# Early gate logits for the sixth batch, and separate pools for the value buffers and the raw second weights

## The chip, the cores and the metric

The kernel runs on one core of one Trainium2 chip. A core has a matrix engine (TensorE, PE in the rows; its weight loads are PEld), a vector engine (VectorE, DVE), a scalar engine (ScalarE, ACT), a general engine (GpSimd, POOL) and a queue engine (SyncE, SP) that issues transfers; GpSimd issues transfers too, the indexed ones. Each engine executes its own instructions in order, and waits on semaphores for the others. The metric is the device time of one execution in microseconds, the median of the runs shown.

## What is computed

An attention by landmarks (eight batches, eight heads, 576 positions, 64 channels; 32 landmarks, a pseudo-inverse by six iterations) makes 4608 rows of 512 numbers; a mixture of eight experts takes each row to the one expert with the largest gate logit.

```
attn = (sm(q, k_lm) @ Z @ sm(q_lm, k) @ v)        # Z: six steps of 2Z - Z Bm Z
x = attn.transpose(0, 2, 1, 3).reshape(B * S, H * D)
logits = x @ w_gate
expert_idx = argmax(logits, axis=1); gate_w = softmax(logits)[expert_idx]
for e in range(E):
    mask = expert_idx == e
    h = maximum(x[mask] @ w1[e], 0); out[mask] = gate_w[mask] * (h @ w2[e])
```

## The kernel before

The work has two halves. The attention runs in 18 periods (`period(i)`); a unit is half a batch (four heads). Unit i is loaded and transposed in period i (`front`), multiplied with the landmarks in i + 1 (`middle`), with the values in i + 2 (`values`); the batch's inverse is iterated in periods 2b + 3 and 2b + 4 (`back`: `chain`, its squarings on L321, then `apply`, which makes the tile w on L364), and its rows come out in 2b + 5 and 2b + 6 (`final`). Inside a period the streams are merged, and a scheduler orders the instructions of each engine at build time, so that any change of the text can move others.

`final` (L374 to L400) goes through the six row blocks j of a batch. For each it makes two products of 96 rows by 264 columns (L388): 256 columns of the row and 8 of the gate logits, two banks of PSUM. ACT copies each to `xrow` (L389), DVE copies and adds the logits (L392, L393), SP stores the row block to `xs`. Only after the last block does `tokens` run: it takes the largest logit, counts the tokens of each expert with seven small products (L569 to L572), and makes the places `l_at` (L583) at which six indexed transfers of GpSimd (`scatter`, L594), 96 tokens each, write the token numbers to the table `order`. `scatter` is a list of work that the next period executes.

The last two batches, 6 and 7 (the seventh and eighth), go another way. `logits` (L402) makes the gate logits alone, six products of 192 columns (L411), transposes them on DVE (L415) and runs `tokens` at once, so that the places are known before the rows; `ended` then makes the rows (L432). Behind the periods stands a hand-written part: the fetch of the second weights of the first expert (L783, `raw1`, four transfers of 512 KB), `scattered` for batch 5, then logits, rows and scatters of batch 6, then of batch 7, with the splits of `raw1` (`whi` on ACT L797, `wlo` on DVE L798) and the first slot's expert product (L853) between them. When all scatters have landed, GpSimd gathers the table (L643), PE turns it (L657), and from it the addresses of all later rows come (L821). From there a loop over slots of 128 rows does up product, ReLU, down product.

The tile pools matter in one way. A pool opened where closed pools lay waits for the tiles of all pools that it overlaps. Here `raw1`, `whi1` and `wlo1` are one pool of 48 KB per partition, opened over the load buffers (`a_ld`: `ld_k`, `ld_q`, `ld_v`) and the transposed ones (`T_k`, `T_q`); another, `e_work` (`buf`, `xt`, `xg`, `h`, `ht`), lies over `T_q` and the work tiles of `middle` and `values`. The first write into such a pool therefore waits for the last product of `values` of the last unit (L263).

In what follows a name with a number in brackets is a batch, as w(6), and the squarings of a batch are counted from 0.

Of the kernel before, what the change touches and what calls it, by code (L numbers as in the profile page):

```python
# [12 lines left out]
F32 = mybir.dt.float32  # L13
# [8 lines left out]
B, H, S, D = 8, 8, 576, 64  # L22
M = 32
P96, J = 96, 6
NT = B * S
DM, NE, DF = 512, 8, 1024
# [34 lines left out]
class Attention:  # L61


    def __init__(self, tc, ctx, front, psum, q, k, v, wg):
        self.tc, self.nc = tc, tc.nc
        nc = self.nc
        self.q, self.k, self.v = q, k, v
        pool = lambda n, b, c=ctx: c.enter_context(tc.tile_pool(name=n, bufs=b))
# [5 lines left out]
        self.row = pool("a_row", 3)  # L74
        self.lg = pool("a_lg", 2)
        self.ld = pool("a_ld", 2, front)
        self.tr = pool("a_tr", 2, front)
        self.wk = pool("a_wk", 2, front)
        self.p_tp, self.p_sc, self.p_fr, self.p_ch, self.p_fi = psum
        self.rows, self.loads, self.banks = [], {}, []  # L80
        c = self.const
# [26 lines left out]
    def load(self, i, names):  # L108
        b, g = divmod(i, 2)
        for n in names:  # L110
            t = self.src[i, n] = self.ld.tile([P96, 4, J * D], F32, name=f"ld_{n}")
            m = 2 if i < 2 else 4
            for h in range(0, 4, m):
                self.loads[n] = self.nc.sync.dma_start(out=t[:, h:h + m], in_=getattr(self, n)[b, 4 * g + h:4 * g + h + m].rearrange("h (p j) d -> p h (j d)", j=J))
# [260 lines left out]
    def final(self, b):  # L375
# [24 lines left out]
                yield  # L400
        yield from sort

    def logits(self, b, room):

        nc = self.nc
        ats, w = self.fin[b]
        pl = self.p_fi.tile([128, 512], F32, name="ps_fi")
        for g in range(2):
            at = ats[g].rearrange("p (a b t c) -> p t b a c", a=2, b=J // 2, t=3)
            for t in range(3):  # L410
                nc.tensor.matmul(pl[32 * t:32 * t + 32, :32 * J].rearrange("p (b a c) -> p b a c", a=2, b=J // 2),  # L411
                                 lhsT=w[:, g, QUAD - 32:], rhs=at[:, t], start=g == 0, stop=g == 1, tile_position=(0, 32 * t))
        yield
        lt = room[:P96, :32 * J]
        nc.vector.transpose(out=lt, in_=pl[:P96, :32 * J])  # L415
        yield from self.tokens(b, range(J), lt.rearrange("p (j e) -> p j e", j=J)[:, :, 32 - NE:])
# [22 lines left out]
    def period(self, i, nb, extra=()):  # L439

        n = 2 * nb
# [14 lines left out]
        for lag, stage, units in ((3, self.back, 26), (5, self.final, 20)):  # L456
            b, h = divmod(i - lag, 2)
            if 0 <= b < nb and (lag, b) not in ((3, nb - 1), (5, nb - 2)):
                if h == 0:
                    self.two[lag, b] = stage(b)  # L460
                half = units // 2 + 1
                streams.append((self.part(self.two[lag, b], 99 if h else half), half, BOOST[lag]))
        if i == n:
# [282 lines left out]
class Experts:  # L746
# [11 lines left out]
        self.hi, self.lo = [None, None], [None, None]  # L758

    def weights(self, ctx, i):  # L760
        p = ctx.enter_context(self.tc.tile_pool(name=f"e_w{i}", bufs=1))
        self.raw[i] = p.tile([128, self.chunks[i], self.width[i]], F32, name=f"raw{i}")
        self.hi[i] = p.tile([128, self.chunks[i], self.width[i]], F32R, name=f"whi{i}")
        self.lo[i] = p.tile([128, self.chunks[i], self.width[i]], F32R, name=f"wlo{i}")

# [186 lines left out]
def moe(tc, q, k, v, wg, w1, w2, out):  # L952
    nc = tc.nc
    with ExitStack() as ctx, ExitStack() as late:
# [9 lines left out]
        with ExitStack() as front:  # L964
            attention = Attention(tc, ctx, front, psum, q, k, v, wg)
            attention.tokens, attention.groups = routing.tokens, routing.groups
            attention.xs = [xs[S * b:S * b + S].rearrange("(p j) c -> p j c", j=J) for b in range(B)]
            routing.ident = attention.ident
            routing.room = {EARLY: front.enter_context(tc.tile_pool(name="r_ids", bufs=1)).tile([16, REC * 128], F32, name="ids_early")}
            for i in range(2 * B + 2):  # L970
                extra = []
# [18 lines left out]
        b = B - 1  # L990
# [88 lines left out]
```

## Time and profile before

| | before |
|---|---|
| median of three runs | 688.84 us (688.47 to 696.65) |
| the profiled execution | 688.39 us, of which the span is 686.6 us |
| PE busy | 647.9 us (94%) |
| DVE, ACT, POOL busy | 520.8, 398.9, 343.9 us (76%, 58%, 50%) |
| mean granted TensorE clock | 0.966 |
| chain that ended last | PE 46% of the span (all of it the expert products), DMA 4%, issue 3%, DVE 1%, POOL 1% |

The page's share of busy time averages over two unlike halves: the attention with many short instructions on all engines up to about 250 us, and the expert loop behind it. Times below are microseconds from the start of the span. In a timeline row, the number in square brackets is the engine's idle time ahead of the row and what ended it. Each matrix product of float32 shows as two rows.

### The profile page before, as it was taken

The numbers are of one execution on the slowest core, as the hardware profiler recorded it, in microseconds if no ns is written. First come the engines' busy times: TensorE is split into PE (matmuls) and PEld (weight loads), VectorE is DVE, ScalarE is ACT, GpSimd is POOL, SyncE is SP. The second block draws the span as 40 slices with busy tenths as digits, with TensorE's granted clock in tenths as the row PEclk, the third lists the DMA queues.
The fourth block names the chain that finished last, engine by engine and source line by source line (L and its number), as shares of the span: only waits on it lengthen the run. The fifth ranks groups of instructions, "written<-read, shape, count | busy, mean of one in ns | idle before, by whom it ended". The sixth has DMA issues, their size and how long they took to land.

```text
span 686.6 us, 13812 instructions
## 1 busy us (share of the span) xinstructions
PE 647.9 (94%) x4511; PEld 509.9 (74%) x4511; DVE 520.8 (76%) x1359; ACT 398.9 (58%) x983; POOL 343.9 (50%) x372
## 2 busy tenths in 40 slices
PE   7899989998898996989999999999999999999996
PEld 4666767666576774768888888888888888888884
DVE  4887967989778677668689699866789699766753
ACT  5776667575645373345567567554567567444542
POOL 4554556575364273777545546344444536441231
PEclk9998999998879897999999999999999999999999
DMA  9996877776442441273145143211144143310110
GB/s 228 294 279 160 207 187 171 178 197 200 111 120 65 137 132 43 73 258 112 62 163 176 56 158 117 107 52 49 45 169 157 59 158 107 118 48 32 32 51 30
DMA packets 46362, 87.50 MB, mean 127 GB/s; under 512 B 7983, under 2 KB 26415, under 8 KB 46192
## 3 DMA queue, kind: packets, MB, share of 16 engines
q1 hardware_dynamic: 36336, 65.30, 33.1%
q0 software_dynamic: 9920, 21.02, 9.7%
q8 instruction: 38, 0.62, 0.4%
q14 instruction: 68, 0.56, 0.3%
HBM read 64.77 MB, written 22.05 MB: 126 GB/s over the span
## 4 chain that ended last, share of the span: by engine, by line
PE 46%; DMA 4%; issue 3%; DVE 1%; POOL 1%; ACT 0%; POOLq 0%; DVEq 0%
PE ps_fi L853 12%; PE ps_ch L853 12%; PE ps_tp L853 11%; PE ps_fr L853 11%; DMA xg<-xs,read 4%; DVE h L873 0%; POOL out_dram L884 0%; POOL xg L821 0%; DVE buf L834 0%; DVE ht L839 0%; ACT ht L836 0%; POOLq L919 0%; POOLq L884 0%; DVEq L834 0%; DVEq L810 0%
## 5 line engine op out<-in xcount | busy, mean ns | idle before, releaser
L884 POOL DMA_INDIRECT out_dram<-buf,write x38 | 38.8, 1020 | 166.4 <-ACTq L810 140.7
L821 POOL DMA_INDIRECT xe<-xs,read x84 | 87.5, 1042 | 25.7 <-issue 24.1
L821 POOL DMA_INDIRECT xg<-xs,read x80 | 83.7, 1046 | 31.3 <-issue 21.8
L853 PE MATMUL ps_fr<-whi,ht 128*128 128x512 f32 x304 | 96.4, 398 | 0.0
L853 PE MATMUL ps_ch<-whi,ht 128*128 128x512 f32 x304 | 94.3, 391 | 2.2 <-ACTq L810 2.2
L836 ACT CAST ht<-buf 128x512 fp32r<-128x512 f32 x76 | 47.1, 621 | 74.9 <-DVE buf L834 73.9
L873 DVE TENSOR_SCALAR h<-ps_tp 32x256 f32<-32x256 f32 x152 | 64.1, 422 | 27.5 <-PE ps_tp L853 25.0
L853 PE MATMUL ps_tp<-whi,xt 128*128 128x512 f32 x304 | 83.2, 395 | 1.5 <-ACTq L810 1.5
L873 DVE TENSOR_SCALAR h<-ps_fi 32x256 f32<-32x256 f32 x144 | 60.7, 422 | 28.9 <-PE ps_fi L853 26.5
L871 ACT ACTIVATE h<-ps_tp 32x256 f32<-32x256 f32 x152 | 57.3, 377 | 36.6 <-PE ps_tp L853 32.9
L853 PE MATMUL ps_fi<-whi,xt 128*128 128x512 f32 x288 | 78.1, 393 | 0.0
L871 ACT ACTIVATE h<-ps_fi 32x256 f32<-32x256 f32 x144 | 54.3, 377 | 34.8 <-PE ps_fi L853 31.1
L853 PEld LDWEIGHTS ps_ch<-whi,ht 128*128 128x128 f32 x304 | 56.9, 188 | 15.2 <-ACTq L810 3.1
L853 PEld LDWEIGHTS ps_fr<-whi,ht 128*128 128x128 f32 x304 | 58.0, 191 | 13.1 <-DVE ht L839 0.5
L853 PEld LDWEIGHTS ps_tp<-whi,xt 128*128 128x128 f32 x304 | 56.9, 188 | 14.3 <-ACTq L810 1.9
L853 PEld LDWEIGHTS ps_fi<-whi,xt 128*128 128x128 f32 x288 | 54.1, 188 | 11.8
L853 PE MATMUL ps_fr<-wlo,ht 128*128 128x512 f32 x152 | 60.4, 397 | 0.0
L594 POOL DMA_INDIRECT order<-i_tok,l_at x48 | 45.7, 952 | 27.7 <-issue 11.5
L853 PE MATMUL ps_ch<-wlo,ht 128*128 128x512 f32 x152 | 59.4, 391 | 0.0
L839 DVE TENSOR_TENSOR ht<-buf,ht 128x512 fp32r<-128x512 f32 x76 | 51.0, 691 | 3.8 <-ACT ht L836 0.2
L798 DVE TENSOR_TENSOR wlo<-raw,whi 128x512 fp32r<-128x512 f32 (+1 forms) x64 | 49.8, 833 | 4.8 <-ACT whi L797 2.4
L834 DVE STREAM_TRANSPOSE buf<-h 128x512 f32<-128x512 f32 x76 | 49.7, 692 | 4.9 <-DMA out_dram<-buf,write 1.0
(274 smaller groups left out, 1325.2 us busy)
## 6 DMA issues: line engine op xcount, KB each, us to landing
raw<-in_moe_w_dram SPq DMA_DIRECT2D x48, 512.0 KB, 5.3
ld_k<-in_k_dram SPq DMA_DIRECT2D x14, 576.0 KB, 5.9
ld_q<-in_q_dram SPq DMA_DIRECT2D x14, 576.0 KB, 7.4
ld_v<-in_v_dram SPq DMA_DIRECT2D x14, 576.0 KB, 4.9
xs<-xrow SPq DMA_DIRECT2D x40, 192.0 KB, 3.3
order<-zero SPq DMA_DIRECT2D x8, 288.0 KB, 9.5
xe<-xs,read POOLq DMA_INDIRECT x84, 2.8
xg<-xs,read POOLq DMA_INDIRECT x80, 2.6
```

The costliest lines, as they stand in the source:

```text
L594: self.nc.gpsimd.indirect_dma_start(out=self.places[n + j], out_offset=bass.IndirectOffsetOnAxis(ap=at[:, j:j + 1], axis=0), in_=self.tok[ ...
L798: (engine or nc.vector).tensor_tensor(out=l, in0=x, in1=h.bitcast(F32), op=ALU.subtract)
L821: self.nc.gpsimd.indirect_dma_start(out=x[:, t, :], out_offset=None, in_=src.rearrange("n (q c) -> (n q) c", q=4), in_offset=bass.Indirect ...
L834: nc.vector.transpose(out=x.rearrange("p c (t j) -> p t c j", t=4), in_=src[:, :, 32 * c:32 * c + 128].rearrange("p t (c i) -> p t c i", c=4))
L836: nc.scalar.copy(out=hi[:, c:c + 4, :], in_=x)
L839: nc.vector.tensor_tensor(out=lo[:, c:c + 4, :], in0=x, in1=hi[:, c:c + 4, :].bitcast(F32), op=ALU.subtract)
L853: nc.tensor.matmul(ps[c // 512] if type(ps) is list else ps[:, c // 512], lhsT=x0[:, a, :], rhs=w[:, a, c:c + 512], start=a == 0 and j == ...
L871: nc.scalar.activation(out=dst, in_=src, func=AF.Relu)
L873: nc.vector.tensor_scalar(out=dst, in0=src, scalar1=0.0, scalar2=None, op0=ALU.max)
L884: nc.gpsimd.indirect_dma_start(out=self.outs[s], out_offset=bass.IndirectOffsetOnAxis(ap=at, axis=0), in_=y, in_offset=None, bounds_check= ...
```

## The change

Batch 5's rows come from a new function, `sorted`, in place of `final`: first the logits alone (`logits`, six products of 192 columns into one bank), then the six row blocks, each with two products of 256 columns into one bank, one copy by ACT of 512 columns instead of two of 256, and one step of `tokens` behind each block. The 12 small copies and adds of DVE are gone; one transpose by DVE into a small tile (`a_room`) stands for them. `tokens` of batch 5 now ends during period 15, so its scatters fall to period 16 instead of the hand-written part. The value buffers get a pool of their own (`a_lv`), and `raw1` one apart from `whi1` and `wlo1`. No tile but `ids_early` changes its address (by 768 bytes); `raw1` lies over `ld_k` and `ld_q` as before, but now waits only for the pool of these two.

```
         self.ld = pool("a_ld", 2, front)
+        self.lv = pool("a_lv", 2, front)
...
-            t = self.src[i, n] = self.ld.tile([P96, 4, J * D], F32, name=f"ld_{n}")
+            t = self.src[i, n] = (self.lv if n == "v" else self.ld).tile([P96, 4, J * D], F32, name=f"ld_{n}")
...
+    def sorted(self, b, room):
+
+        nc = self.nc
+        sort = self.logits(b, room)
+        next(sort)
+        yield
+        ats, w = self.fin.pop(b)
+        for j in range(J):
+            x = self.row.tile([P96, DM], F32, name="xrow")
+            n = self.at_col(j)
+            po = self.p_fi.tile([128, 512], F32, name="ps_fi")
+            for g in range(2):
+                nc.tensor.matmul(po[:P96, 4 * D * g:4 * D * g + 4 * D], lhsT=ats[g][:, n:n + 96], rhs=w[:, g, :4 * D], start=True, stop=True)
+                if g == 0:
+                    yield
+            nc.scalar.copy(out=x.rearrange("p (q c i) -> p c q i", q=4, c=4), in_=po[:P96].rearrange("p (c q i) -> p c q i", c=4, q=4))
+            nc.sync.dma_start(out=self.xs[b][:, j, :], in_=x)
+            next(sort, None)
+            yield
...
-                    self.two[lag, b] = stage(b)
+                    self.two[lag, b] = stage(b) if (lag, b) != (5, nb - 3) else self.sorted(b, self.room)
...
+        p = ctx.enter_context(self.tc.tile_pool(name=f"e_raw{i}", bufs=1))
+        self.raw[i] = p.tile([128, self.chunks[i], self.width[i]], F32, name=f"raw{i}")
         p = ctx.enter_context(self.tc.tile_pool(name=f"e_w{i}", bufs=1))
-        self.raw[i] = p.tile([128, self.chunks[i], self.width[i]], F32, name=f"raw{i}")
...
+            attention.room = front.enter_context(tc.tile_pool(name="a_room", bufs=1)).tile([P96, 32 * J], F32, name="room")
```

Lines of the changed kernel stand 1 to 23 higher: its L432 (logits), L453 (rows of batches 6 and 7), L590 to L593 (counts), L264 (values), L322 (squarings), L856 (turn) are L411, L432, L569 to L572, L263, L321, L834 of before.

PE, from the first product of batch 5's rows in period 15, before:

```order
L388 MATMUL ps_fi<-w,at 96x264
L321 MATMUL ps_ch<-bt 128x160 x2
L388 MATMUL ps_fi<-w,at 96x264
L173 MATMUL ps_sc<-T_q,lm_k 32x288 x8
L125 MATMUL ps_tp<-ident,ld_q 128x96 x3
L271 MATMUL ps_fr<-ident,st 64x128
L125 MATMUL ps_tp<-ident,ld_q 128x96 x3
L388 MATMUL ps_fi<-w,at 96x264
L321 MATMUL ps_ch<-rp 128x128 x2
L125 MATMUL ps_tp<-ident,ld_q 128x96 x3
L277 MATMUL ps_fr<-wg,yt 32x8 x4
L388 MATMUL ps_fi<-w,at 96x264
```

and of the changed kernel:

```order
L432 MATMUL ps_fi<-at,w 32x192 x6
L322 MATMUL ps_ch<-bt 128x160 x2
L416 MATMUL ps_fi<-w,at 96x256 x2
L174 MATMUL ps_sc<-T_q,lm_k 32x288 x6
L126 MATMUL ps_tp<-ident,ld_q 128x96 x3
L174 MATMUL ps_sc<-T_q,lm_k 32x288 x2
L272 MATMUL ps_fr<-ident,st 64x128
L126 MATMUL ps_tp<-ident,ld_q 128x96 x3
L416 MATMUL ps_fi<-w,at 96x256 x2
L322 MATMUL ps_ch<-rp 128x128 x2
L126 MATMUL ps_tp<-ident,ld_q 128x96 x3
L278 MATMUL ps_fr<-wg,yt 32x8 x4
```

The logits stand ahead of everything; further on, up to the products of landmarks of the last unit (L178, L179 of the changed kernel), PE has the seven counts and ten row products instead of six row products ahead of it.

DVE, from the first instruction that writes into `e_work` (`buf` 4091 to 4093 of before), before:

```order
L834 STREAM_TRANSPOSE buf_4091<-xe_144 128x4x4x32
L581 TENSOR_TENSOR l_t<-l_t,l_oh 96x48
L834 STREAM_TRANSPOSE buf_4092<-xe_145 128x4x4x32
L339 TENSOR_TENSOR rp<-rp,ps_tp 128x2x32
L582 TENSOR_REDUCE l_mx<-l_t 96x6
L415 STREAM_TRANSPOSE buf_4093<-ps_fi 96x192
L839 TENSOR_TENSOR xt_4094<-buf_4091,xt_4094 128x512
L583 CAST l_at<-l_mx 96x6
L554 TENSOR_REDUCE l_mx<-buf_4093 96x6
L839 TENSOR_TENSOR xt_4095<-buf_4092,xt_4095 128x512
L555 TENSOR_TENSOR buf_4093<-buf_4093,l_mx 96x6x8
L339 TENSOR_TENSOR rp<-rp,ps_tp 128x2x32
```

and of the changed kernel (L436 is the transpose of logits, here of batch 6; L820 is `wlo`; L340 is L339 of before):

```order
L436 STREAM_TRANSPOSE buf_4091<-ps_fi 96x192
L856 STREAM_TRANSPOSE buf_4089<-xe_144 128x4x4x32
L856 STREAM_TRANSPOSE buf_4090<-xe_145 128x4x4x32
L340 TENSOR_TENSOR rp<-rp,ps_tp 128x2x32
L575 TENSOR_REDUCE l_mx<-buf_4091 96x6
L820 TENSOR_TENSOR wlo_4082<-raw_4077,whi_4081 128x512
L576 TENSOR_TENSOR buf_4091<-buf_4091,l_mx 96x6x8
L820 TENSOR_TENSOR wlo_4082<-raw_4077,whi_4081 128x512
L340 TENSOR_TENSOR rp<-rp,ps_tp 128x2x32
L820 TENSOR_TENSOR wlo_4082<-raw_4077,whi_4081 128x512
```

The transpose of batch 6's logits has moved ahead of the two turns of the first slots, the steps of `tokens` of batch 5 are gone from here, and three subtractions `wlo` have come in ahead of the rest of `tokens` of batch 6; the row that makes its `l_oh` (L564 of before, L585 now) follows after two `xt` subtractions and the two masks L342.

On SP the four transfers of `raw1` stand after the second of the six stores of batch 5 instead of after the sixth, and wait for the last transpose of `ld_q` instead of the last product with `ld_v`. On GpSimd the six scatters of batch 5 stand one `a` product (L236) earlier.

## Rows read from the trace of the kernel before

**Rows 1.** Busy time of each engine by stretches of 50 us: PE, PEld, DVE, ACT, POOL, then granted clock, share of DMA engines, GB/s. One stretch across the join of attention and experts, one of the expert loop.

```profile
250.00:300.00 50.00, 42.80 (x176) 33.37 (x175) 33.67 (x91) 20.20 (x45) 31.45 (x34) 0.90 0.26 74
350.00:400.00 50.00, 50.00 (x220) 40.96 (x219) 42.04 (x79) 31.50 (x68) 23.33 (x22) 1.00 0.39 129
```

**Rows 2.** The chain that ended last, in order of time: first and last of its 58 PE pieces (start, length, what).

```profile
305.42 5.75 PE ps_ch L853 x24
...
619.17 5.53 PE ps_fi L853 x24
```

**Rows 3.** Timeline of PE where the table's transposes stand (start, length, operation).

```profile
264.76 1.07 PE L657 MATMUL ps_fi<-ident,r 43*128 43x43 f32 x4 [5.67 <-DVE r L653]
...
268.48 1.05 PE L853 MATMUL ps_fr<-whi,ht 128*128 128x512 f32 x2
...
269.76 1.05 PE L853 MATMUL ps_fr<-whi,ht 128*128 128x512 f32 x2
...
273.01 0.61 PE L853 MATMUL ps_fr<-whi,ht 128*128 128x512 f32 x2
...
273.69 0.61 PE L853 MATMUL ps_fr<-whi,ht 128*128 128x512 f32 x2
```

**Rows 4.** Stretches around that wait, columns as in rows 1.

```profile
259.00:266.00 7.00, 1.33 (x6) 0.96 (x5) 3.07 (x8) 4.22 (x10) 0.80 (x1) 0.66 0.28 57
266.00:271.00 5.00, 5.00 (x12) 3.60 (x12) 4.63 (x12) 0.00 (x0) 2.91 (x4) 0.50 0.10 30
```

**Rows 5.** Timeline of GpSimd: the first scatter of batch 5, the first and the last of batch 6, the first of batch 7, the gather of the table.

```profile
233.93 1.25 POOL L594 DMA_INDIRECT order<-i_tok,l_at  x1 [10.88 <-DVE l_mx L554]
...
241.60 0.92 POOL L594 DMA_INDIRECT order<-i_tok,l_at  x1 [0.30 <-DVE l_at L583]
...
247.96 1.05 POOL L594 DMA_INDIRECT order<-i_tok,l_at  x1 [0.30 <-issue]
249.32 0.92 POOL L594 DMA_INDIRECT order<-i_tok,l_at  x1 [0.31 <-issue]
...
258.90 0.90 POOL L643 DMA_INDIRECT ht<-order,s_at  x1 [2.17 <-issue]
```

**Rows 6.** Timeline of DVE: the masks of batch 7 and the third squaring's sum of batch 6 behind them, w(6), the first turn, l_oh(6), the first `wlo`, w(7), l_at(7).

```profile
212.15 2.91 DVE L297 TENSOR_TENSOR bt<-bt,m 128x128 f32<-128x128 f32 x2
...
215.93 0.20 DVE L339 TENSOR_TENSOR rp<-rp,ps_ch 128x64 f32<-128x64 f32 x1
...
228.01 0.42 DVE L364 TENSOR_TENSOR w<-ps_ch,m 128x256 f32<-128x256 f32 x1
...
231.07 0.71 DVE L834 STREAM_TRANSPOSE buf<-xe 128x512 f32<-128x512 f32 x1 [2.11 <-PE ps_fr L263]
...
236.35 0.20 DVE L564 TENSOR_TENSOR l_oh<-i_rev,l_m 96x48 bf16<-96x48 f32 x1
...
240.42 0.69 DVE L798 TENSOR_TENSOR wlo<-raw,whi 128x512 fp32r<-128x512 f32 x1 [2.26 <-DMA xs<-xg]
241.03 0.24 DVE L583 CAST l_at<-l_mx 96x6 int32<-96x6 f32 x1
241.10 0.74 DVE L364 TENSOR_TENSOR w<-ps_ch,m 128x256 f32<-128x256 f32 x2
...
248.13 0.16 DVE L583 CAST l_at<-l_mx 96x6 int32<-96x6 f32 x1
```

**Rows 7.** Timeline of PE: landmarks of the last unit, the first three of the twelve rows of logits(6), the last product with the values, rows of batch 6, counts of batch 6, first product behind them, logits(7).

```profile
209.48 0.23 PE L178 MATMUL ps_tp<-lm_k,lm_q 64*32 64x32 f32 x4
...
230.56 0.54 PE L411 MATMUL ps_fi<-at,w 128*32 128x192 f32 x3
230.66 0.31 PE L263 MATMUL ps_fr<-ld_v,ct 96*32 96x64 f32 x1
...
231.99 2.02 PE L432 MATMUL ps_fi<-w,at 128*96 128x256 f32 x4
...
236.69 0.20 PE L569 MATMUL ps_fi<-l_oh,tri 96*96 96x48 bf16 x1
...
243.56 0.85 PE L411 MATMUL ps_fi<-at,w 128*32 128x192 f32 x12
244.34 1.10 PE L432 MATMUL ps_fi<-w,at 128*96 128x256 f32 x4
245.28 1.03 PE L432 MATMUL ps_sc<-w,at 128*96 128x256 f32 x4
```

**Rows 8.** Stretches of the end of the attention, columns as in rows 1.

```profile
227.05:230.45 3.40, 3.40 (x37) 2.98 (x37) 1.86 (x7) 0.17 (x1) 0.00 (x0) 0.50 0.00 0
230.45:233.90 3.45, 3.45 (x20) 1.91 (x20) 2.83 (x10) 1.85 (x4) 0.00 (x0) 0.50 0.44 116
```

**Rows 9.** Groups of instructions on DVE from 229 to 246 us (busy us, mean ns of one, idle ahead).

```profile
L798 DVE TENSOR_TENSOR wlo<-raw,whi 128x512 fp32r<-128x512 f32 x3 | 2.0, 689 | 2.3 <-DMA xs<-xg 2.3
L834 DVE STREAM_TRANSPOSE buf<-xe 128x512 f32<-128x512 f32 x2 | 1.4, 704 | 2.1 <-PE ps_fr L263 2.1
L839 DVE TENSOR_TENSOR xt<-buf,xt 128x512 fp32r<-128x512 f32 x2 | 1.3, 660 | 0.0
```

**Rows 10.** Transfers of the raw second weights: the time from issue to landing, from the view of that tile (225 to 262 us).

```profile
DMA to landing us min/median/max: 3.9/5.4/7.0
```

**Rows 11.** The same for the transfers on the tensor `xs`, 200 to 262 us.

```profile
DMA to landing us min/median/max: 2.1/2.3/3.2
```

## The prediction

> **What bounds the kernel now.** I read the busy time by stretches first. In the expert loop PE is busy all of a stretch at full clock; across the join it misses 7.2 us of 50 [rows 1]. The chain of waits says the same: 58 pieces of expert products follow one another without a gap from 305.42 us to 619.17 + 5.53 = 624.70 [rows 2]. Nothing of the change touches that loop, so its length stays, and the question is only when it begins.
>
> Its beginning hangs on the token table. PE stands still for 5.67 us ahead of the transposes of the table (L657) and resumes at 264.76 [rows 3]. The reader should go back from there on GpSimd: the gather of the table is issued at 258.90, behind the last of six scatters of batch 7, which begin at 249.32 [rows 5]. What the first of these waited for is seen in two rows: l_at(7) is done at 248.13 + 0.16 = 248.29 [rows 6], and GpSimd's last scatter of batch 6 ends at 247.96 + 1.05 = 249.01 [rows 5]. So GpSimd's own queue held it, by 0.7 us only; right behind stands l_at(7). And l_at(7) hangs on PE: from the counts of batch 6 (L569, 236.69) to logits(7) (243.56) PE goes without a gap through rows of batch 6 and first-slot products [rows 7].
>
> The order behind the scatters is the same in both kernels, so the whole execution moves by what the first scatter of batch 7 moves, plus what the clock does on the way. The profiled execution took 688.39 us, 0.45 below the median of 688.84; sums are made against 688.4.
>
> **The change, part by part.**
>
> *Batch 5's scatters leave the tail.* GpSimd is free for 10.88 us ahead of them [rows 5], so they hide in that idle time. This gives the 0.7 us above and no more, because behind it l_at(7) decides.
>
> *The early fetch of raw1.* DVE waits 2.26 us for the landed weights, and w(7) starts only at 241.10 [rows 6]. But w(7) is done at 241.84, and PE reaches logits(7), which reads it, at 243.56 [rows 6, 7]: 1.7 us later, with PE busy in between. I cost this part at nothing; its cover is that slack.
>
> *The smaller work.* The row products shrink from 264 to 256 columns and the small DVE steps go; none of that is on the path alone. Added on PE are the six products for logits(5): 0.85 us at full clock, as logits(7) shows, 1.43 at half, as logits(6) shows (230.56 to 231.99) [rows 7].
>
> *The new order in period 15.* Up to the landmarks of the last unit (L178, 209.48 before) PE now has the logits (1.4), two more pairs of row products (two times 0.94, from the start of one pair at 244.34 to the next at 245.28 [rows 7]) and the counts (0.3 to 0.6) ahead of it: 3.6 to 3.9 us. Batch 7's chain starts that much later, but catches up, since its squarings follow each other at their own pace. Batch 6's chain gains: its third sum (L339, 215.93) stood behind batch 7's masks of 2.91 us [rows 6], and now stands ahead of them. Going through the new order with the durations of before, I find that sum at about 215.1, the next two 0.9 and 0.3 earlier, and then, where the tokens of batch 5 are gone from DVE, w(6) at 225.8 instead of 228.01 and logits(6) at 226.75 instead of 230.56. This replay is good to perhaps 1.5 us.
>
> *The last product with the values.* Behind logits(6) PE has the first four row products (1.9), the rest of the values (0.45) and a squaring (0.55); with the logits' 0.85 that is 3.75 us at full clock. Call the end of the last values product T. Before it is 230.66 + 0.31 = 230.97 [rows 7]; after it is 226.75 + 3.75 = 230.5.
>
> *The new order on DVE behind T.* The transpose of logits(6) is the first write into the `e_work` pool and must wait for T, as the first turn does now (2.11 us, 231.07) [rows 6]. From there to l_oh(6) DVE has in its queue: that transpose (0.3), two turns (0.70 each), three `wlo` (0.69 each), two `xt` subtractions (0.66 each) [rows 9], and some ten short ones with two masks (1.9 together): 6.9 us. Before, l_oh(6) came at 236.35, 5.3 us behind the first turn [rows 6], because the `wlo` stood behind it. The counts of batch 6 on PE wait for l_oh(6), and queued behind them are the rows of batch 6, the product that makes w(7), and logits(7).
>
> *The sum.* From the counts to logits(7) 243.56 - 236.69 = 6.87 [rows 7]; from there to the end of l_at(7) 248.29 - 243.56 = 4.73 [rows 6, 7]; to the scatter 0.3, GpSimd's gap between two issues [rows 5]. So the first scatter of batch 7 is at T + 0.1 + 6.9 + 6.87 + 4.73 + 0.3 = T + 18.9 = 249.4, against 249.32: 0.1 later. What was won up to T is spent in DVE's queue behind it.
>
> *The clock.* Behind T PE has some 1.2 us of work in 7. What such a pause does is shown once in this trace: after 5.67 us of waiting the granted clock is 0.50 of the full 2.4 GHz from 266 to 271 us [rows 4], and a group of three products goes from 1.28 (268.48 to 269.76) to 0.68 (273.01 to 273.69) when it is back [rows 3]. Four such groups cost 2.4 us. I take 2.5 for the stretch of 6.87 us, which is then no longer at the full clock that it had. Below it could cost nothing (the clock stays), above it could cost 6.9 (the whole stretch at half); I take the one case that the trace shows, and leave the upper end to the range.
>
> Forecast: 688.4 + 0.1 + 2.5 = **691.0 us**. The half clock that before falls on 227.05 to 233.90 [rows 8] is spent there on logits(6) and the first rows; in this forecast these run at full clock.
>
> **The rivals.**
>
> *The clock stays full behind T.* Then the sum is 0.1, 688.5 us. For it: PE is not wholly idle there. Against it: 1.2 us of work in 7 is nearer to the idle stretch after which the clock fell [rows 3, 4] than to a busy one.
>
> *Half clock on both sides of T.* If the clock falls at 227.05 as before, the 3.75 us ahead of T take about 7.2, by the logits' 1.43 against 0.85 and four row products' 2.02 against 1.10 [rows 7, 8]; T is 234.0, and with the 2.5 behind it the time is 694.5. For it: by the replay the squarings ahead of T alternate with DVE's sums as before, so PE pauses there as often.
>
> *The other side: batch 6's chain is ready sooner than the replay says.* The place is w(6) on DVE, the price is one for one. If logits(6) comes 2 us earlier (224.7) and the clock stays, T is 228.5 and the scatter at 247.4: 686.5 us. It decides from T = 230.4 down at full clock. For it: the small DVE steps of batch 5's rows and its seven counts are gone from the way to logits(6). Against it: three PE steps that now stand ahead of batch 7's chain.
>
> *The stores stuck behind the weights.* raw1's four transfers are now issued at about 208, with batch 5's third store behind them on the same queue, and ACT's sixth copy of that batch waits for that store to free its buffer. If it lands with the last of the weights (7.0 us after an issue near 210.4 [rows 10], 217.4), ACT stands 1.1 us behind its turn at 216.35, and the squarings of both batches with it: 692.1. Against it: stores that followed the weights before landed within 3.2 us [rows 11]. The Trainium skill (DMA: Bandwidth & Descriptors, section "Queues, rings and completion order") says that each DMA engine takes the descriptors of one ring in order; by that rule a store issued last would be read last, and this rival would hold. The trace does not bear the rule out as a delay: 3.2 us is less than the weights' 5.4 median.
>
> That the early scatters do nothing at all is no rival of its own: it is the 0.7 us in the first case.
>
> **How the numbers follow.** Forecast 0.38; clock stays 0.24; half clock on both sides 0.17; sooner 0.14; stores stuck 0.07. The range goes from 685.5, the sooner case with 1 us of the replay's error, to 695.4, half clock on both sides with 0.9 of it: outside lie a third of the sooner case and of the slowest, 0.10, and whatever is in no case. The likeliest alone spans 689.5 to 692.5, by the replay's 1.5. What a measurement of this kernel can tell from no change is about 2%, 13.8 us; no case comes near. Faster by more 0.01, within 0.97, slower by more 0.02.
>
> **What would show it.** In the profile of the changed kernel: raw1 issued near 208 us and no wait for it on DVE (the early fetch works and gains nothing); batch 5's scatters ahead of 223 us; logits(6) near 226.8; DVE waiting for the last values product, then 6.9 us to l_oh(6); PE nearly idle for that long, and granted clock 0.50 in some of the 8 us behind it; the first scatter of batch 7 near 252 and waiting for l_at(7), no longer for GpSimd; the expert loop unchanged at 5.5 us a piece. The forecast is wrong if logits(6) comes before 225 or after 229, if l_oh(6) comes sooner than 6 us after the last values product, or if the wait ahead of the table's transposes shrinks so far that the clock holds there, which would give back up to 2.5 us.

## The result and the profile after

The changed kernel takes 697.23 us (median of 20 runs, 694.87 to 700.93) against 687.86 us; the ratio is 1.0143, 95% interval 1.0125 to 1.0161. It is 9.4 us slower, where 2.6 was forecast. The profiled execution took 698.87 us, its span 697.1. Disturbed runs are left out of all ratios.

The expert loop is what it was, and begins 10.1 us later. The chain of waits of the changed kernel (start, length, what):

```profile
315.53 5.75 PE ps_ch L875 x24
...
629.66 5.52 PE ps_fi L875 x24
```

From the first piece to the end of the last it takes 629.66 + 5.52 - 315.53 = 319.65 us, before 624.70 - 305.42 = 319.28 [rows 2]. The loss lies ahead of it. The timeline of PE in the changed kernel: w(5)'s product, the landmarks of the last unit, logits(6), the last products with the values, counts of batch 6, logits(7).

```profile
197.61 1.02 PE L362 MATMUL ps_ch<-st,bdz 128*128 128x72 f32 x4
...
214.56 0.23 PE L179 MATMUL ps_tp<-lm_k,lm_q 64*32 64x32 f32 x4
...
234.69 1.26 PE L432 MATMUL ps_fi<-at,w 128*32 128x192 f32 x12
...
238.97 0.31 PE L264 MATMUL ps_fr<-ld_v,ct 96*32 96x64 f32 x6
...
245.72 0.25 PE L590 MATMUL ps_fi<-l_oh,tri 96*96 96x48 bf16 x1
...
254.28 0.85 PE L432 MATMUL ps_fi<-at,w 128*32 128x192 f32 x12
```

And of GpSimd: the first scatters of batches 5, 6 and 7.

```profile
216.20 0.95 POOL L615 DMA_INDIRECT order<-i_tok,l_at  x1 [0.17 <-DVE c_sm L203]
...
247.70 0.94 POOL L615 DMA_INDIRECT order<-i_tok,l_at  x1 [20.09 <-DVE l_at L604]
...
259.29 0.91 POOL L615 DMA_INDIRECT order<-i_tok,l_at  x1 [4.53 <-DVE l_at L604]
```

In the kernel before w(5)'s product stood at 196.37; this row was not shown:

```profile
196.37 1.02 PE L361 MATMUL ps_ch<-st,bdz 128*128 128x72 f32 x4
```

So 1.24 us of the 10.0 by which batch 7's first scatter moved (259.29 against 249.32 [rows 5]) were there already at that product. Up to it the order of the instructions is the same in both kernels, and executions of three later versions have it at 196.82, 197.47 and 199.28: one execution differs from another by as much. The rest lies in six stretches that follow one another, from w(5)'s product to that scatter. Each number is the difference of two starts in these rows or in [rows 5, 7]; T is the end of the last values product. The forecast column is the prediction's own working.

| stretch, us | before | forecast | after |
|---|---|---|---|
| w(5)'s product to landmarks | 13.11 | 16.9 | 16.95 |
| landmarks to logits(6) | 21.08 | 13.5 | 20.13 |
| logits(6) to T | 0.41 | 3.75 | 4.59 |
| T to counts of batch 6 | 5.72 | 7.0 | 6.44 |
| counts to logits(7) | 6.87 | 9.4 | 8.56 |
| logits(7) to first scatter of batch 7 | 5.76 | 5.0 | 5.01 |
| sum | 52.95 | 55.6 | 61.68 |

One stretch holds the error: landmarks to logits(6), 6.6 us over the forecast. What happens there is seen on ACT, whose timeline of the changed kernel reads:

```profile
217.86 0.46 ACT L259 COPY ct<-ps_tp 96x384 f32<-96x384 f32 x1
221.22 0.58 ACT L419 COPY xrow<-ps_fi 96x512 f32<-96x512 f32 x1 [2.90 <-DMA xs<-xrow]
221.70 0.48 ACT L259 COPY ct<-ps_tp 96x384 f32<-96x384 f32 x1
222.07 0.69 ACT L231 ACTIVATE a<-a 128x576 f32<-128x576 f32 x1
222.66 0.36 ACT L338 COPY rp<-ps_ch 128x256 f32<-128x256 f32 x1
```

ACT's sixth copy of batch 5 waits 2.90 us for a store of `xrow` to free its buffer. The queue of SyncE in the changed kernel (start, length, transfers) and the line of the stores show which:

```profile
206.75 3.30 SPq L420 DMA_DIRECT2D xs<-xrow  x2
210.32 2.28 SPq L805 DMA_DIRECT2D raw<-in_moe_w_dram  x4
212.78 9.35 SPq L420 DMA_DIRECT2D xs<-xrow  x4
```

```profile
  ACT xrow L419: 2.9, 1
...
DMA to landing us min/median/max: 2.1/2.2/8.4
```

The third store is issued at 212.78, right behind the weights, and lands 8.4 us later, at 221.2. (The 2.2 is the median of the three stores of the six whose landing the profile tells.) By the trace's semaphore counts, the four weights and the three stores behind them begin to be complete in the order of their issue, the last weight at 218.43 and the third store at 218.87. Behind ACT's copy stand the softmax's exponential (L231) and the squaring's copy (L338), and DVE waits for the first with the squaring's next sum queued behind:

```profile
217.02 0.21 DVE L340 TENSOR_TENSOR rp<-rp,ps_ch 128x64 f32<-128x64 f32 x1
...
222.80 0.75 DVE L234 TENSOR_REDUCE a_sm<-a 128x18 f32<-128x576 f32 x1 [2.77 <-ACT a L231]
...
223.92 0.18 DVE L340 TENSOR_TENSOR rp<-rp,ps_ch 128x64 f32<-128x64 f32 x1
```

PE pauses with them, for ACT's second copy `ct`, and its clock falls. The row of that pause, and stretches of the changed kernel, columns as in rows 1:

```profile
222.23 0.87 PE L264 MATMUL ps_fr<-ld_v,ct 96*32 96x64 f32 x24 [2.26 <-ACT ct L259]
```

```profile
205.20:220.90 15.70, 14.78 (x164) 10.39 (x162) 10.84 (x51) 7.99 (x22) 12.53 (x13) 1.00 0.72 222
221.95:235.55 13.60, 11.94 (x100) 10.11 (x103) 10.17 (x29) 4.84 (x13) 2.62 (x3) 0.50 0.07 17
242.45:249.20 6.75, 4.79 (x19) 3.83 (x20) 4.81 (x22) 1.21 (x3) 1.20 (x2) 0.50 0.01 2
```

Before, the clock was at half (1.2 of 2.4 GHz) from 227.05 to 233.90, 6.85 us [rows 8]. Now it is at half for 13.6 us ahead of T, while the squarings of batch 6 run, and for another 6.75 behind it.

### The profile page after: what moved, and what is told of

Same layout as the page of the kernel before. It is cut to its first block, busy times and chain, and to the rows that moved or that the text cites. A ratio compares the mean times of both kernels' runs of the same rounds, so it can differ in the third digit from the quotient of the medians.

```text
span 697.1 us, 13815 instructions
## 1 busy us (share of the span) xinstructions
PE 654.2 (94%) x4523; PEld 513.8 (74%) x4523; DVE 518.9 (74%) x1348; ACT 397.9 (57%) x977; POOL 343.0 (49%) x372
## 4 chain that ended last, share of the span: by engine, by line
PE 46%; DMA 3%; issue 3%; POOL 1%; DVE 1%; ACT 0%; POOLq 0%; DVEq 0%
PE ps_fi L875 12%; PE ps_ch L875 12%; PE ps_fr L875 11%; PE ps_tp L875 11%; DMA xe<-xs,read 3%; DVE h L895 0%; POOL xg L843 0%; POOL out_dram L906 0%; POOL xe L843 0%; DVE buf L856 0%; DVE ht L861 0%; ACT ht L858 0%; POOLq L941 0%; POOLq L906 0%; DVEq L856 0%
## 5 line engine op out<-in xcount | busy, mean ns | idle before, releaser
L856 DVE STREAM_TRANSPOSE buf<-h 128x512 f32<-128x512 f32 x76 | 49.7, 690 | 5.3 <-DMA out_dram<-buf,write 1.5
L820 DVE TENSOR_TENSOR wlo<-raw,whi 128x512 fp32r<-128x512 f32 (+1 forms) x64 | 49.9, 834 | 2.5 <-ACT whi L819 2.4
```

Source lines behind the costliest of these rows:

```text
L820: (engine or nc.vector).tensor_tensor(out=l, in0=x, in1=h.bitcast(F32), op=ALU.subtract)
L856: nc.vector.transpose(out=x.rearrange("p c (t j) -> p t c j", t=4), in_=src[:, :, 32 * c:32 * c + 128].rearrange("p t (c i) -> p t c i", c=4))
```

## The experiments

Two theories of the loss. **Q**: the store queued behind the weights stops ACT, ACT stops DVE and PE, and the pause brings the clock down early. **O**: the work now ahead of the landmarks makes batch 7's chain late, and the rest follows. Two more came up on the way: **V**, the last values product now stands behind logits(6) and rows; **D**, DVE's queue behind that product.

Beside fifteen of the eighteen runs the kernel before took 739 to 744 us, not 688; these are read by their ratio alone, against each other, and the last section shows what their profile looks like. Three runs (`row_extra_c`, `vals_first_b`, `wlo_behind`) stand beside a kernel before of 688 to 689 us, as the prediction does.

The profiles of the fifteen show why they say little of Q. In all eleven with `sorted` ACT stands still for 4.7 to 5.6 us soon after the landmarks, with a releaser ("remote") that the profile cannot name; the four with `final` have no such stand there. ACT of the changed kernel among them, `after_again`:

```profile
250.48 0.37 ACT L338 COPY rp<-ps_ch 128x256 f32<-128x256 f32 x1 [4.75 <-remote]
...
252.62 0.59 ACT L419 COPY xrow<-ps_fi 96x512 f32<-96x512 f32 x1
```

The sixth copy follows without a wait. So none of the eleven shows Q's wait, not even `after_again`, and their ratios hold a cost that the runs at 688 us do not have.

### A buffer more, or the weights behind the stores

`row_extra` (and `_b`, `_c`) gives the sixth row block a tile of its own; the order on the queues stays.

```
-            x = self.row.tile([P96, DM], F32, name="xrow")
+            x = self.row.tile([P96, DM], F32, name="xrow") if j < J - 1 else self.spare
...
+            attention.spare = front.enter_context(tc.tile_pool(name="a_spare", bufs=1)).tile([P96, DM], F32, name="xspare")
```

> The changed kernel with one thing more: the sixth row block of batch 5 is copied into a buffer of its own, so ACT's copy no longer waits for the third store; the order on all queues stays, the weights still stand ahead of the third store. Theory Q (a store queued behind the weights stops ACT, ACT stops PE and DVE, and the pause brings the clock down at 221 instead of 227): ACT's wait of 2.9 us at 221.2 is gone, the last values product comes 3 to 6 us sooner than 239.3, time 691 to 694.5 against 697.2. Theory O (the logits, row products and counts now ahead of the landmarks of the last unit put batch 7's chain 4 us late and the rest follows from that; ACT's wait lies in slack): the wait goes, the time stays within 1 us of 697.2.

> The kernel with a buffer of its own for the sixth row block again, now beside the changed kernel. Theory Q: faster than the changed kernel by 3 to 6 us, ACT never waits for a store of batch 5. Theory O: within 1 us of the changed kernel.

> The changed kernel with a buffer of its own for the sixth row block of batch 5, once more. On a chip like that of the prediction (kernel before 688 us), theory Q: no wait of ACT for a store, the clock holds at 221, the last values product 3 to 6 us sooner than 239.3, ratio 1.005 to 1.010 instead of 1.014. Theory O: ratio 1.013 to 1.015. On chips like those of the first nine runs (740 us) the ratio is 1.012 as twice before, and nothing new is told apart.

`row_extra`: 1.0113 (1.0061 to 1.0165); `row_extra_b`: 1.0127 (1.0076 to 1.0178), against 1.0178 (1.0120 to 1.0237) for the changed kernel beside it (`after_again`). These intervals overlap and decide nothing. `row_extra_c` does: 694.12 us against 689.44, ratio 1.0071 (1.0044 to 1.0099), where the changed kernel has 1.0143 (1.0125 to 1.0161). About 5 us of the 9.4 are gone with one tile, and the order of the instructions is that of the changed kernel on every engine. Its ACT, PE, first scatter of batch 7 and clock:

```profile
217.06 0.57 ACT L419 COPY xspare<-ps_fi 96x512 f32<-96x512 f32 x1
```

```profile
196.82 1.02 PE L362 MATMUL ps_ch<-st,bdz 128*128 128x72 f32 x4
...
213.75 0.23 PE L179 MATMUL ps_tp<-lm_k,lm_q 64*32 64x32 f32 x4
...
230.41 1.28 PE L432 MATMUL ps_fi<-at,w 128*32 128x192 f32 x12
...
234.71 0.31 PE L264 MATMUL ps_fr<-ld_v,ct 96*32 96x64 f32 x6
...
241.38 0.25 PE L590 MATMUL ps_fi<-l_oh,tri 96*96 96x48 bf16 x1
...
249.98 0.85 PE L432 MATMUL ps_fi<-at,w 128*32 128x192 f32 x12
```

```profile
254.99 0.92 POOL L615 DMA_INDIRECT order<-i_tok,l_at  x1 [4.58 <-DVE l_at L604]
```

```profile
204.20:224.45 20.25, 17.91 (x212) 12.97 (x211) 16.25 (x68) 11.56 (x31) 15.89 (x17) 1.00 0.61 186
224.55:231.30 6.75, 6.75 (x54) 5.61 (x56) 4.83 (x12) 1.87 (x5) 0.00 (x0) 0.50 0.00 0
```

ACT does not wait, the clock falls near 224.5 instead of 221.9 and stays down for 6.75 us ahead of T instead of 13.6, and landmarks to logits(6) take 230.41 - 213.75 = 16.66 us instead of 20.13. The six stretches add up to 254.99 - 196.82 = 58.17 us instead of 61.68; each of the other five differs by less than 0.1 us. Theory Q holds for half the loss. In this pair of executions the wait costs 3.5 us, 2.9 of which are its own length; how much of the rest the longer half clock makes was not separated.

`raw_after` (and `_b`) puts the weights behind the sixth store:

```
-            nc.sync.dma_start(out=self.xs[b][:, j, :], in_=x)
+            self.stored = nc.sync.dma_start(out=self.xs[b][:, j, :], in_=x)
...
-            experts.fetch(1, routing.first[0:1, 0:1])
+            with tc.issue_after(attention.stored.ins):
+                experts.fetch(1, routing.first[0:1, 0:1])
```

> The changed kernel with the four transfers of the weights issued behind the sixth store of batch 5 instead of behind the second; they still wait only for the pool of ld_k and ld_q. Theory Q: the third store lands in 2 to 3 us, ACT does not wait, the time is that of the kernel with the extra buffer, 691 to 694.5. Theory O: 697.2 within 1 us. If the early fetch is worth something by itself, this one is 1 to 2 us above the kernel with the extra buffer.

> The changed kernel with the weights' transfers behind the sixth store of batch 5. Theory Q: no wait of ACT, the ratio is that of the extra buffer, 1.004 to 1.010. If the fetch itself (its traffic beside the stores and scatters) costs: between that and 1.014.

1.0151 (1.0095 to 1.0207) and 1.0105 (1.0069 to 1.0142), one above and one below the two of the extra buffer in this kind of run: not told apart from it or from the changed kernel. ACT waits for no store, but here none of the eleven does.

### One half of the change alone

`sorted_only` keeps the new function and puts back the pools; `pools_only` keeps the pools and puts back `final`.

```
-            t = self.src[i, n] = (self.lv if n == "v" else self.ld).tile([P96, 4, J * D], F32, name=f"ld_{n}")
+            t = self.src[i, n] = self.ld.tile([P96, 4, J * D], F32, name=f"ld_{n}")
...
-        p = ctx.enter_context(self.tc.tile_pool(name=f"e_raw{i}", bufs=1))
-        self.raw[i] = p.tile([128, self.chunks[i], self.width[i]], F32, name=f"raw{i}")
         p = ctx.enter_context(self.tc.tile_pool(name=f"e_w{i}", bufs=1))
+        self.raw[i] = p.tile([128, self.chunks[i], self.width[i]], F32, name=f"raw{i}")
```

```
-                    self.two[lag, b] = stage(b) if (lag, b) != (5, nb - 3) else self.sorted(b, self.room)
+                    self.two[lag, b] = stage(b)
...
-            attention.room = front.enter_context(tc.tile_pool(name="a_room", bufs=1)).tile([P96, 32 * J], F32, name="room")
```

> The changed kernel with the pools of before: the values are loaded into the load pool, the raw second weights lie in one pool with their splits, so their fetch waits again for the last values product. The new function for batch 5's rows stays. Theory Q: 691 to 694.5, since no store stands behind the weights. Theory O: 696 to 698, since the order in period 15 is that of the changed kernel.

> The changed kernel with the pools of before: no early fetch, so no store stands behind the weights, and the three wlo cannot stand ahead of the masks of batch 6 (the weights land 7 us behind the last values product). Theory Q: no wait of ACT for a store. With theory V the ratio is that of the extra buffer, 1.005 to 1.009; with theory D it is 1.000 to 1.004, because the masks of batch 6 come 5.3 us behind the first turn as in the kernel before.

> The kernel before with the two new pools alone: batch 5's rows are made as before, and the weights come to stand between batch 5's stores on the queue. Theory Q: the stores behind the weights hold ACT here too (it has three row buffers), 690 to 695 against 687.9. Theory O: no difference from before by more than 1 us, since the order in period 15 is that of before.

> The kernel before with the two new pools alone, again. Theory Q: a store of batch 5 behind the weights lands after 5 us or more and ACT waits for it, 2 to 6 us slower than the kernel before. Theory O: within 1 us of the kernel before.

> The kernel before with the two new pools alone; three of the weights' transfers stand between the first and the second, and one between the second and the third, of its last six stores. Theory Q: ACT waits for a store (1.3 us in both earlier profiles) and the time is 1 to 4 us above the kernel before, ratio 1.002 to 1.006. If the wait is all in slack: 0.998 to 1.001.

`sorted_only`: 1.0120 (1.0063 to 1.0178) and 1.0110 (1.0057 to 1.0163). `pools_only`: 1.0060 (0.9999 to 1.0121), 1.0041 (1.0002 to 1.0080), 1.0066 (1.0032 to 1.0100). In this kind of run each half alone is slower than the kernel before, `pools_only` just so. In all three profiles of `pools_only` ACT waits for a store; its row in `pools_only_c`:

```profile
245.11 0.37 ACT L390 COPY xrow<-ps_fi 96x256 f32<-96x256 f32 x1 [1.38 <-DMA xs<-xrow]
```

So the early fetch brings Q's wait without the new function too; that this wait is what makes `pools_only` slower was not tested. `sorted_only` is no faster than `row_extra` in the same kind of run. With 4.8 us of stand in both its profiles, its ratio decides neither between Q and O nor between V and D, whose 1.000 to 1.004 it does not meet.

### The place of the last values product

`vals_first` is the extra buffer, and logits(6) and the first rows of batch 6 wait on PE's order for the last product with the values:

```
-                nc.tensor.matmul(py[32 * h:32 * h + 32, :D], lhsT=ct[:, j, 32 * h:32 * h + 32],
+                self.valued = nc.tensor.matmul(py[32 * h:32 * h + 32, :D], lhsT=ct[:, j, 32 * h:32 * h + 32],
...
-            soon(l6, 1)
+            with tc.issue_after(attention.valued.ins):
+                soon(l6, 1)
             experts.early()
-            step(six, 4)
+            with tc.issue_after(attention.valued.ins):
+                step(six, 4)
```

> The kernel with the extra buffer, and with logits(6) and the first rows of batch 6 put behind the last values product on PE, so that the products of the new order no longer stand between the two. In the kernel with the extra buffer logits(6) ran at 230.4 as in the kernel before (230.6), yet the last values product ended at 235.0 instead of 231.0. Theory V (what is left of the loss is the place of the last values product, for which DVE's first write into the new work pool waits): it ends at 232 to 233.5, the time falls by 1.5 to 3 us below the kernel with the extra buffer, ratio 1.002 to 1.005. Theory D (DVE's queue behind that product, three wlo ahead of the masks of batch 6, is what is left): the time stays, since that queue stays or grows; ratio 1.006 to 1.009.

> The kernel with the extra buffer and logits(6) behind the last values product, again, for a chip like that of the prediction. There, theory V: the last values product ends at 232 to 233.5 instead of 235.0, ratio 1.002 to 1.005 instead of 1.007; theory D: 1.006 to 1.009. On the slower chips the ratio was 1.0038 against 1.0113 and 1.0127 for the extra buffer alone, which speaks for V; there nothing new is expected.

`vals_first`: 1.0038 (1.0004 to 1.0072), beside 1.0113 and 1.0127 for the extra buffer alone; but `all_three` below, which contains this edit, has 1.0113 and 1.0066 in the same kind of run. `vals_first_b`: 691.32 against 687.82 us, 1.0050 (1.0028 to 1.0072). Its timeline of PE:

```profile
199.28 1.02 PE L362 MATMUL ps_ch<-st,bdz 128*128 128x72 f32 x4
...
233.50 0.87 PE L264 MATMUL ps_fr<-ld_v,ct 96*32 96x64 f32 x24 [0.57 <-ACT ct L259]
234.15 1.50 PE L432 MATMUL ps_fi<-at,w 128*32 128x192 f32 x12
...
240.93 0.22 PE L590 MATMUL ps_fi<-l_oh,tri 96*96 96x48 bf16 x1 [0.43 <-DVE l_oh L585]
```

T, at 234.37, is 35.09 us behind w(5)'s product; with the buffer alone it was 235.02 - 196.82 = 38.20. At 688 us the ratio fell by 0.0021, 1.4 us; the two intervals overlap, and the ratio just meets V's upper bound of 1.005. V is likely, not shown as a time.

### DVE's queue, and what the clock does with the gain

`wlo_behind` adds to that: the last three `wlo` stand behind l_oh(6) on DVE.

```
-        v.tensor_tensor(out=oh, in0=bj(self.rev), in1=be(m8), op=ALU.is_equal)
+        self.hot = v.tensor_tensor(out=oh, in0=bj(self.rev), in1=be(m8), op=ALU.is_equal)
...
             soon(l6, 2)
+            hot = routing.hot
...
-            done(split)
+            with tc.issue_after(hot.ins):
+                done(split)
```

> The kernel with the extra buffer and logits(6) behind the last values product, and now with the last three wlo of the weights put behind l_oh(6) on DVE. In the run before, l_oh(6) stood at 240.68, 6.3 us behind the last values product, with three wlo (1.9 us) ahead of it and PE nearly idle that long. Theory D (that queue is part of what is left): l_oh(6) comes 4 to 4.8 us behind the product, the time falls by 1.5 to 3 us, ratio 1.001 to 1.003 instead of 1.005. If the counts then wait for something else (PE's own work between the product and the counts is 5.5 us in that order): less than 1 us, ratio 1.004 to 1.006.

691.72 against 688.59 us, 1.0044 (1.0027 to 1.0062): no step from 1.0050, although T to the counts fell to 4.45 us. Its PE, the clock of `vals_first_b`, and its own:

```profile
197.47 1.02 PE L362 MATMUL ps_ch<-st,bdz 128*128 128x72 f32 x4
...
230.73 0.54 PE L264 MATMUL ps_fr<-ld_v,ct 96*32 96x64 f32 x24 [0.57 <-ACT ct L259]
...
235.72 0.22 PE L590 MATMUL ps_fi<-l_oh,tri 96*96 96x48 bf16 x1 [1.25 <-DVE l_oh L585]
...
249.49 0.85 PE L432 MATMUL ps_fi<-at,w 128*32 128x192 f32 x12
```

```profile
227.00:237.15 10.15, 9.58 (x85) 7.42 (x85) 7.49 (x17) 4.24 (x10) 0.00 (x0) 0.50 0.00 0
```

```profile
207.00:237.65 30.65, 26.26 (x323) 19.37 (x322) 27.18 (x89) 18.10 (x48) 14.65 (x15) 1.00 0.41 124
237.75:247.90 10.15, 9.58 (x28) 7.40 (x28) 2.75 (x15) 1.34 (x4) 5.54 (x6) 0.50 0.22 62
```

Measured from w(5)'s product, the counts come 3.4 us sooner than in `vals_first_b` (38.25 against 41.65 us) and logits(7) 2.1 us later (52.02 against 49.90). In that execution the half clock fell wholly behind T, on 237.75 to 247.90, where `vals_first_b` had it mostly ahead, and the counts' way to logits(7) took 13.77 us instead of 8.25. These are single executions; that the clock took the gain away is likely, not shown.

### The landmarks sooner

`rows_behind` puts the products of row blocks 3 to 5 of batch 5 behind the landmarks, from the changed kernel; `all_three` (and `_b`) adds that to `wlo_behind`. For it batch 5's stream does 7 of its 20 steps in the first of its two periods.

```
+                if (lag, b) == (5, nb - 3):
+                    half = 20 - 7 if h else 7
...
-            self.nc.tensor.matmul(ps[32 * h:32 * h + 32, :], lhsT=ql[:64, h, :], rhs=kl[:64, h, :], start=True, stop=True,
+            self.marks = self.nc.tensor.matmul(ps[32 * h:32 * h + 32, :], lhsT=ql[:64, h, :], rhs=kl[:64, h, :], start=True, stop=True,
...
+                with self.tc.issue_after(self.marks.ins) if j > 2 else nullcontext():
```

> The changed kernel itself, as the measure for the others of this call, since the first four ran on a chip on which the kernel before took 741 us instead of 688. Theory Q and theory O both expect the ratio of 1.014 to the kernel before, a third store of batch 5 that lands after about 8 us, a wait of ACT of 2 to 3 us for it, and the last values product 6 to 9 us later than in the kernel before.

> The changed kernel with the row products of blocks 3 to 5 of batch 5 put behind the landmarks of the last unit on PE (logits, counts and blocks 0 to 2 stay ahead); the queue of the weights stays. Theory O: the landmarks come 1.9 us sooner against the rest of the program and batch 7's chain with them, 2 to 3 us faster than the changed kernel. Theory Q: the store is still held for 8 us and ACT with it (its sixth copy now stands further back, so its wait may shrink by up to 1 us); within 1 us of the changed kernel.

> The kernel of the run before (extra buffer, logits(6) behind the last values product, wlo behind l_oh(6)), and with the row products of blocks 3 to 5 of batch 5 behind the landmarks of the last unit. In the run before, l_oh(6) came 5 us sooner than before that, but logits(7) did not come sooner: PE ran at half clock from 237 to 247, and batch 7's chain had to end first. Theory O for the rest (the landmarks come 3.8 us late, batch 7's chain with them, and w(7) ends the way): the landmarks come 1.9 us sooner against the first product of period 15, the time falls by 1 to 2.5 us, ratio 1.001 to 1.003. Theory C (what is left is half clock that a pause of PE brings somewhere in these 40 us whatever the order): within 1 us of the run before, ratio 1.003 to 1.006, with 7 us or more of half clock between 215 and 260.

> The same kernel again, since the run before fell on a chip on which the kernel before takes 743 us. On a chip like that of the prediction, theory O: ratio 1.001 to 1.003, landmarks 1.9 us sooner; theory C: 1.003 to 1.006, with 7 us or more of half clock between 215 and 260. On the other kind of chip: 1.011 as before.

`after_again` 1.0178 (1.0120 to 1.0237), `rows_behind` 1.0212 (1.0162 to 1.0262), `all_three` 1.0113 (1.0065 to 1.0161) and 1.0066 (1.0024 to 1.0109), all beside a kernel before of 740 to 743 us. None shows a gain from earlier landmarks, and all four hold the stand of ACT; at 688 us this was not run. `before_again` gave a profile alone:

> The kernel before itself, for its profile beside the others. Every theory expects the order of the kernel before and no wait of ACT for a store of batch 5. On the chip of the first eight runs: 740 us, and engines that stand still here and there with nothing in the profile that they wait for; the question is whether the kernel before has such a stand at the landmarks of the last unit (5 us in the changed kernel and its variants there). On a chip like that of the prediction: 688 us.

## Why the prediction was wrong

**Right.** What bounds the kernel, that its loop stays, and where its start hangs. The scatters of batch 5 left the tail (216.20 on), and batch 7's first now waits for l_at(7), as forecast. The new order in period 15 cost 16.95 - 13.11 = 3.8 us up to the landmarks, where 3.6 to 3.9 was worked out. Behind T the stretches came out at 6.44 + 8.56 + 5.01 = 20.0 us where 18.9 + 2.5 was forecast, with the clock at 0.50 from 242.45 to 249.20. And the early fetch gained nothing. Too wide was the 2% that a measurement was said to tell from no change: the interval is 1.0125 to 1.0161.

**Wrong: the step "the new order in period 15", which let logits(6) come at 226.75.** It came at 234.69. The replay took each engine's queue with the durations of before and let ACT's sixth copy start in its turn. That this copy waits for a store was written down as a rival ("the stores stuck behind the weights"), with a chance of 0.07 and a price of 1.1 us. It is what happened: a wait of 2.90 us, and the run with one more buffer takes 3.5 us away between the profiled executions and about 5 between the medians. The landing was put at 217.4, with the last of the weights, and was at 221.2.

The evidence against the rival was a view with a gap. Rows 11 were read as stores that landed within 3.2 us. That view counts only transfers whose landing the profile tells: 6 of the 18 stores in its window, and the 3.2 is an indexed gather's (L821); the longest of the six took 3.1. The two stores right behind the weights are not among the six. The view of transfers shows it for the kernel before; 234 to 236 us has no time behind the store, 241 to 242 us has one:

```profile
xs<-xrow SPq DMA_DIRECT2D x1, 192.0 KB
...
xs<-xrow SPq DMA_DIRECT2D x1, 192.0 KB, 3.1
```

The trace does hold that landing: the semaphore of the store issued at 234.65 counts its sixteen parts from 239.96 to 243.03. That is 8.4 us, as in the changed kernel. Before, no copy of ACT waited for it. The rival's own sum, with 8.4 us for a store issued 0.65 us behind the last weight (as in the changed kernel; that is near 211.05), gives a landing at 219.45 and a wait of 3.1 us, an estimate. The rule that the prediction set against the row (the Trainium skill, DMA: Bandwidth & Descriptors, section "Queues, rings and completion order": each DMA engine consumes the descriptors of one ring in order) would have given this rival, and both traces agree with it: 8.4 us for the store right behind the weights.

**Also wrong: the clock ahead of T.** The forecast gave these stretches full clock. Even without ACT's wait it was at half from near 224.5 in `row_extra_c`, and landmarks to logits(6) took 16.66 us there where 13.5 was forecast. The rival "half clock on both sides of T" (0.17, 694.5 us) has the time of `row_extra_c` (694.12 us), in part by luck: it put the half clock on logits(6) and the rows, 7.2 us up to T, which took 4.61, while the half clock lay on the squarings ahead of logits(6) and on logits(6). The two rivals were counted as alternatives; in the changed kernel both came true, and the half clock ahead of T is twice as long as without the wait, 13.6 us against 6.75.

**What stays open.** Of the loss, about 5 us went with the buffer (1.0143 to 1.0071, intervals apart), 1.4 to 1.9 more with the last values product ahead of logits(6) (1.0071 to 1.0050 or 1.0044; likely, the intervals overlap). The last 3 us (0.0044 of 688) may be the later landmarks, which these three versions keep, or where the half clock falls; neither is shown, and no version beat the kernel before.

## What to carry to other kernels

When a large transfer is moved ahead on a queue, look at what the next small transfer on it holds: a store that frees a buffer is a wait of the engine that fills it. Before a view's minimum, median and maximum are used as evidence, count the transfers that they cover, and ask whether the one in question is among them. Rivals that can come true together should be priced together. And where a replay with old durations forecasts a gain, first ask for each buffer who frees it in the new order.

## What the runs showed of the hardware that was not expected

The same kernel took 688 us beside some runs and 740 beside others. `before_again` (746.8 us span) shows where such time goes. PE and ACT of its period 15:

```profile
237.24 0.27 PE L263 MATMUL ps_fr<-ld_v,ct 96*32 96x64 f32 x1 [1.14 <-issue]
237.94 0.27 PE L263 MATMUL ps_fr<-ld_v,ct 96*32 96x64 f32 x1 [0.43 <-issue]
```

```profile
240.07 0.40 ACT L126 COPY T_k<-ps_tp 128x288 f32<-128x288 f32 x1 [15.19 <-remote]
```

```profile
225.00:239.00 14.00, 5.07 (x29) 2.18 (x27) 0.54 (x3) 0.00 (x0) 9.36 (x10) 0.50 0.10 26
```

For 14 us ACT does nothing, PE executes its values products with gaps of up to 1.14 us and no releaser (in `vals_first_b` above 24 of them took 0.87 us in one piece, also at half clock), and only GpSimd works on, with its indexed transfers. The DMA engines are nearly idle (0.10). At its own landmarks this kernel has no stand of ACT; it has another, of 7.17 us, ahead of 287.59. What the engines wait for, the profile does not say, and no run was made to find out.
